# First two batches' queries and keys as six tokens to a partition on 96 partitions, second V ahead of the residual weights, third batch's key casts on ScalarE and its key transposes between the outputs

## Chip, cores, metric

One core of a Trainium2 chip. The metric is the device time of one execution in microseconds; a lower one is better. A kernel's time is the median of its runs; a profiled run adds its trace. In what follows faster or slower needs 2%.

## The reference

Attention in a window of 32 tokens to each side plus 8 global tokens, over 8 batches, 8 heads, 576 tokens of 64 columns; its output is the input of a gated feed-forward network with a residual:

```python
mask = (np.abs(pos[:, None] - pos[None, :]) <= 32) | is_global[:, None] | is_global[None, :]
x = softmax(where(mask, q @ k.T / 8, -1e9)) @ v           # 8 batches, 8 heads, 576 x 64
x = x.transpose(0, 2, 1, 3).reshape(4608, 512)
ffn = (gelu(x @ w_gate) * (x @ w_val)) @ w_out            # 512 -> 1536 -> 512
out = x + sigmoid(x @ w_res) * ffn
```

## The kernel before

It goes through the 4608 tokens in nine chunks of 512. Within a chunk TensorE makes the gate and value products (`g_ps`, `v_ps`), then the residual gate (`r_ps`, weights `wr_t`) and the output (`f_ps`, weights `wo_t`), and between these the scores and values of the next chunk. Global scores (`sg` from queries `qt`, `ss` from keys `kt`) of the next batch come at the end of a chunk's gate products. All weights are loaded in float32 and cast to bf16 in the first 75 us, mostly by GpSimd, in the same queue as the casts of Q, K and V. The first two batches are transposed by TensorE; from the third on, DMA transposes do it. An output product goes through two buffers: VectorE writes it to `prb`, GpSimd adds the residual into `ob`, and SyncE issues the store of `ob`; there are two of each. In the views PE is TensorE, POOL GpSimd, DVE VectorE, ACT ScalarE and SPq the queue of SyncE, which issues most transfers. The first two batches' Q and K were loaded per pair of heads, four tokens to each of 128 partitions, with a tail of 64 tokens (p < 0); the code is shortened:

```python
RPP = 4; SM = RPP * 128; ST = S - SM
def load_raw(b, what, p, eng):
    if p < 0:                                             # 64 tail tokens of all heads
        eng.dma_start(raw[b][what][:, MW:MW + RPP * D],
                      bass.AP(tensor=src.tensor, offset=..., ap=[[S * D, H], [RPP * D, ST // RPP], [1, RPP * D]]))
    else:                                                 # 512 tokens of two heads: 262 KB
        eng.dma_start(raw[b][what][:, PW * p:PW * p + PW].rearrange("c (h n) -> c h n", h=2),
                      src[b, 2 * p:2 * p + 2, 0:SM].rearrange("h (c r) d -> c h (r d)", r=RPP))
...
for p in (0, 1, 2, 3, -1):                                # second batch, after weight pieces 0 to 11
    for what in "kq": load_raw(1, what, p, nc.sync)
...                                                       # chunk 0, j == 5:
load_vraw(1); load_piece(14); load_piece(15)              # 12, 13 = wr_t were issued before
for n in (12, 13): cast_piece(n, POOL)
for c5 in range(5): cast_v(1, c5, POOL)
shift_v(1)
...                                                       # end of chunk 0, then chunk 1
for what in "kq": cast_second(what, POOL)                 # third batch: ten casts ahead of ...
    gpsimd.tensor_tensor(ob, prb, xtok, add)              # ... the four output adds, two prb buffers
    sync.dma_start(out, ob)
turn_qk(2); load_v(2); gather(...)                        # DMA transposes on SyncE, V on GpSimd
```

The softmax here doesn't subtract the row's maximum and nothing guards it: scores larger than these inputs give would overflow.

## Time and profile before

| | kernel before |
|---|---|
| median of the timed runs | 409.08 us (408.6 to 409.57) |
| the profiled run | 412.05 us, span 410.3 us, granted clock 0.996 |
| first gate product | 28.13 us |
| chunk 1 starts (gate product) | 75.75 us |
| chunk 2 starts | 123.04 us |
| chunk 2's start to the end | 287.3 us |

### The profile page before, as it was taken

The numbers are of one execution on the slowest core, as the hardware profiler recorded it, in microseconds if no ns is written. First come the engines' busy times: TensorE is split into PE (matmuls) and PEld (weight loads), VectorE is DVE, ScalarE is ACT, GpSimd is POOL, SyncE is SP. The second block draws the span as 40 slices with busy tenths as digits, with TensorE's granted clock in tenths as the row PEclk, the third lists the DMA queues.
The fourth block names the chain that finished last, engine by engine and source line by source line (L and its number), as shares of the span: only waits on it lengthen the run. The fifth ranks groups of instructions, "written<-read, shape, count | busy, mean of one in ns | idle before, by whom it ended". The sixth has DMA issues, their size and how long they took to land.

```text
span 410.3 us, 8005 instructions
## 1 busy us (share of the span) xinstructions
PE 389.0 (95%) x3136; PEld 204.7 (50%) x3136; DVE 201.2 (49%) x418; ACT 169.1 (41%) x278; POOL 170.8 (42%) x210
## 2 busy tenths in 40 slices
PE   2889999699999999999999999999999999999995
PEld 1554555244654465446544654456445644554442
DVE  6658537136544555345634563466336534463321
ACT  5674590023623363336333533353435343633320
POOL 6788685589326712562256215612600220021012
PEclk9999999989999999999999999999999999999999
DMA  7999999499939974999399938994692320031001
GB/s 228 219 386 355 220 289 240 114 154 170 140 89 113 196 64 88 125 155 115 92 115 168 111 91 108 161 125 81 104 133 54 76 67 0 2 91 54 1 26 77
DMA packets 151830, 53.28 MB, mean 130 GB/s; under 512 B 136368, under 2 KB 140976, under 8 KB 151792
## 3 DMA queue, kind: packets, MB, share of 16 engines
q1 hardware_dynamic: 75840, 42.41, 43.9%
q0 software_dynamic: 75392, 9.84, 37.5%
q8 instruction: 24, 0.39, 0.4%
q10 hardware_dynamic: 560, 0.52, 0.4%
q14 instruction: 14, 0.11, 0.1%
HBM read 39.19 MB, written 9.44 MB: 119 GB/s over the span
## 4 chain that ended last, share of the span: by engine, by line
PE 60%; issue 17%; DMA 12%; POOL 5%; SPq 5%; DVE 1%; POOLq 0%; ACTq 0%
PE v_ps L544 15%; PE g_ps L540 15%; PE f_ps L567 15%; PE r_ps L557 5%; SPq L177 3%; POOL ob L573 3%; PE nd L508 3%; DMA extra<-in_moe_w_val_dram 3%; DMA extra<-in_moe_w_out_dram 2%; DMA wo_t<-in_k_dram 2%; PE sc L464 2%; PE sn L441 2%; DMA ht<-in_q_dram 2%; PE nd L502 1%; PE sg L419 1%
## 5 line engine op out<-in xcount | busy, mean ns | idle before, releaser
L547 ACT ACTIVATE gsb<-g_ps 128x512 bf16<-128x512 f32 x108 | 64.5, 597 | 140.5 <-PE g_ps L540 135.7
L548 DVE SCALAR_TENSOR_TENSOR ht<-gsb,v_ps 128x512 bf16<-128x512 bf16 x108 | 74.0, 686 | 97.1 <-PE v_ps L544 94.2
L573 POOL TENSOR_TENSOR ob<-prb,xtok 128x512 f32<-128x512 f32 x36 | 41.5, 1153 | 187.2 <-DVE prb L571 186.1
L540 PE MATMUL g_ps<-xt,wg_t 128*128 128x512 bf16 x432 | 111.8, 381 | 4.2 <-DVE prb L571 3.5
L544 PE MATMUL v_ps<-xt,wv_t 128*128 128x512 bf16 x432 | 111.8, 381 | 0.1
L567 PE MATMUL f_ps<-wo_t,ht 128*128 128x512 bf16 x432 | 103.6, 379 | 1.0 <-POOL wo_t L137 1.0
L540 PEld LDWEIGHTS <-wg_t 128*128 128x128 bf16 x432 | 42.2, 98 | 54.5 <-issue 5.7
L544 PEld LDWEIGHTS <-wv_t 128*128 128x128 bf16 x432 | 42.5, 98 | 51.9 <-issue 1.6
L567 PEld LDWEIGHTS <-ht 128*128 128x128 bf16 x432 | 39.0, 98 | 40.1 <-issue 1.8
L560 ACT ACTIVATE rsb<-r_ps 128x512 bf16<-128x512 f32 x36 | 21.6, 604 | 74.1 <-PE r_ps L557 74.0
L571 DVE SCALAR_TENSOR_TENSOR prb<-rsb,f_ps 128x512 f32<-128x512 bf16 x36 | 24.7, 685 | 36.9 <-PE f_ps L567 28.7
L471 ACT ACTIVATE pt<-sc 128x512 bf16<-128x512 f32 x72 | 37.4, 610 | 4.0 <-PE sc L464 4.0
L557 PE MATMUL r_ps<-wr_t,xt 128*128 128x512 bf16 x144 | 36.8, 379 | 0.1
L486 DVE TENSOR_TENSOR pt<-pt,maskw 128x512 bf16<-128x512 bf16 x64 | 26.6, 428 | 9.0 <-ACT pt L471 6.9
L91 POOL DMA_DIRECT2D q_st<-in_q_dram x25 | 21.1, 862 | 21.8 <-DMA qt<-q_st 21.4
L99 POOL DMA_DIRECT2D ve<-in_v_dram x30 | 25.4, 862 | 0.0
L522 DVE TENSOR_TENSOR xtok<-nd,rden 128x512 bf16<-128x512 f32 x34 | 23.5, 691 | 1.3
L508 PEld LDWEIGHTS <-pt 128*128 128x128 bf16 x576 | 22.3, 97 | 1.0
L508 PE MATMUL nd<-ve,pt 128*128 128x65 bf16 x320 | 22.3, 193 | 0.0
L91 POOL DMA_DIRECT2D k_st<-in_k_dram x25 | 21.2, 875 | 2.7 <-DMA kt<-k_st 2.0
L521 DVE RECIPROCAL rden<-nd 128x8 f32<-128x8 f32 x34 | 7.0, 207 | 30.4 <-PE nd L508 30.2
L557 PEld LDWEIGHTS <-xt 128*128 128x128 bf16 x144 | 13.4, 97 | 15.1
(136 smaller groups left out, 306.1 us busy)
## 6 DMA issues: line engine op xcount, KB each, us to landing
out_dram<-ob SPq DMA_DIRECT2D x36, 256.0 KB, 2.1
vo<-ve SPq DMA_DIRECT2D x14, 260.0 KB, 5.6
q_st<-in_q_dram POOLq DMA_DIRECT2D x20, 128.0 KB, 5.2
k_st<-in_k_dram POOLq DMA_DIRECT2D x20, 128.0 KB, 6.4
ve<-in_v_dram POOLq DMA_DIRECT2D x18, 128.0 KB, 6.3
wo_t<-in_k_dram SPq DMA_DIRECT2D x8, 256.0 KB, 6.4
extra<-in_moe_w_gate_dram SPq DMA_DIRECT2D x4, 512.0 KB, 8.7
vraw<-in_q_dram SPq DMA_DIRECT2D x8, 256.0 KB, 6.4
```

What stands on the lines that cost most here:

```text
L91: nc.gpsimd.dma_start(dst[0:n, r, :].rearrange("p (h d) -> p h d", d=D), src[b].rearrange("h s d -> s h d")[128 * r:128 * r + n])
L99: nc.gpsimd.dma_start(t[p0:p1, c, :, 0:D], v[b].rearrange("h s d -> s h d")[s0 + p0:s0 + p1])
L471: nc.scalar.activation(mine, sc, ACTF.Exp, bias=0.0, scale=SCALE)
L486: nc.vector.tensor_tensor(m, m, view(maskw, 0, 128, 64 * i0, [[0, 2], [64, 4], [1, 64]]), ALU.mult)
L508: nc.tensor.matmul(nds[h // 4][:, VG * (h % 4):VG * (h % 4) + VG], view(pt, 0, 128, c0, [[1, 128]]), vw, start=False, stop=(h % 4 == 3 and ...
L540: nc.tensor.matmul(g_ps, wg_t[:, kk, 128 * j:128 * j + 128], x[:, kk, :], start=(kk == 0), stop=(kk == NKT - 1))
L544: nc.tensor.matmul(v_ps, wv_t[:, kk, 128 * j:128 * j + 128], x[:, kk, :], start=(kk == 0), stop=(kk == NKT - 1))
L547: nc.scalar.activation(gsb, g_ps, ACTF.Gelu, bias=0.0, scale=1.0)
L548: nc.vector.scalar_tensor_tensor(ht[:, j, :], gsb, 0.5, v_ps, ALU.mult, ALU.mult)
L557: nc.tensor.matmul(r_ps, xt[c % 2][:, kk, 128 * t:128 * t + 128], wr_t[:, kk, :], start=(kk == 0), stop=(kk == NKT - 1))
L567: nc.tensor.matmul(held["f"], ht[:, j, 128 * t:128 * t + 128], wo_t[:, j, :], start=(j == 0), stop=(j == NFF - 1))
L573: nc.gpsimd.tensor_tensor(ob, prb, xtok[c % 2][:, t, :], ALU.add)
```

## The change

Three parts. (1) Q and K of the first two batches are loaded as six tokens to each of 96 partitions, in eight loads of 295 KB, so the eight-head tail loads and their transposes and copies go. (2) The second batch's V is loaded and cast before the residual weights `wr_t`, so that `wo_t`, which waits behind the shift of V, comes earlier. (3) The third batch's keys are cast by ScalarE, so that only five query casts share GpSimd with the output adds, and the key transposes are issued on SyncE in the middle of the four outputs.

```diff
-    RPP = 4
-    SM = RPP * 128
+    RPP = 6
+    PC = S // RPP
...
-        if p < 0:
-            eng.dma_start(raw[b][what][:, MW:MW + RPP * D], ... 8 heads x 16 groups ...)
-        else:
-            eng.dma_start(raw[b][what][:, PW * p:PW * p + PW]..., src[b, 2 * p:2 * p + 2, 0:SM]...)
+        eng.dma_start(raw[b][what][0:PC, PW * p:PW * p + PW].rearrange("c (h n) -> c h n", h=2),
+                      src[b, 2 * p:2 * p + 2].rearrange("h (c r) d -> c h (r d)", r=RPP))
...
-    for n in (12, 13):
+    load_vraw(1)
+    for n in (12, 13, 14, 15):
         load_piece(n)
...
-                    load_vraw(1)
-                    for n in (14, 15):
-                        load_piece(n)
+                    for c5 in range(5):
+                        cast_v(1, c5, POOL)
+                        if c5 == 0:
+                            gather("k", 1)
+                    shift_v(1)
+                    gather("q", 1)
                     for n in (12, 13):
                         cast_piece(n, POOL)
-                    for c5 in range(5):
-                        cast_v(1, c5, POOL)
-                    shift_v(1)
+                    gather("v", 1)
...
-            for what in "kq":
-                cast_second(what, POOL)
+            cast_second("k", 0, NQT, ACT)
...
+            cast_second("q", 0, 1, POOL)
             work_f[3]()                      # output 1
+            turn_qk(2, "k")                  # five key transposes on SyncE
             values(1, 3)
+            cast_second("q", 1, 2, POOL)
             work_f[7]()                      # output 2
+            cast_second("q", 2, NQT, POOL)
...
-            turn_qk(b)
+            turn_qk(b, "q" if c == 1 else "qk")
```

More of the change, by code (lines that the diff above doesn't have):

```diff
@@ L64, in pair_of @@
         return [const.tile(shape, dt, name=f"{name}{i}", tag=f"{name}{i}") for i in range(2)]
-    q_st = const.tile([128, NQT, H * D], BF16, name="q_st", tag="q_st")
-    k_st = const.tile([128, NQT, H * D], BF16, name="k_st", tag="k_st")
+    q_st = const.tile([128, NQT + 1, H * D], BF16, name="q_st", tag="q_st")
+    k_st = const.tile([128, NQT + 1, H * D], BF16, name="k_st", tag="k_st")
     qt = pair_of([128, NP, S], "qt")
@@ L110, in flat32 @@
         return f.bitcast(F32)[:, o:o + 1024]
-    vraw = const.tile([128, 5, 512], F32, name="vraw", tag="vraw")
+    vraw = const.tile([128, 6, 512], F32, name="vraw", tag="vraw")
     extra = const.tile([128, 4, 1024], F32, name="extra", tag="extra")
@@ L137, in cast_piece @@
         copy(pieces[n][1], staged(n))
-    RPP = 4
-    SM = RPP * 128
-    ST = S - SM
+    RPP = 6
+    PC = S // RPP
     PW = 2 * RPP * D
-    MW = NP * PW
     ht32 = ht.rearrange("p a b -> p (a b)").bitcast(F32)
@@ L153, in load_raw @@
         src = {"q": q, "k": k}[what]
-        if p < 0:
-            eng.dma_start(raw[b][what][:, MW:MW + RPP * D],
-                          bass.AP(tensor=src.tensor, offset=src.offset + (b * H * S + SM) * D,
-                                  ap=[[S * D, H], [RPP * D, ST // RPP], [1, RPP * D]]))
-        else:
-            eng.dma_start(raw[b][what][:, PW * p:PW * p + PW].rearrange("c (h n) -> c h n", h=2),
-                          src[b, 2 * p:2 * p + 2, 0:SM].rearrange("h (c r) d -> c h (r d)", r=RPP))
-    for p in (0, 1, -1, 2, 3):
+        eng.dma_start(raw[b][what][0:PC, PW * p:PW * p + PW].rearrange("c (h n) -> c h n", h=2),
+                      src[b, 2 * p:2 * p + 2].rearrange("h (c r) d -> c h (r d)", r=RPP))
+    for p in range(NP):
         load_raw(0, "k", p, nc.sync)
@@ L185 @@
     place2 = {"q": [vraw[:, r, :] for r in range(NQT)],
-              "k": [extra[:, r // 2, 512 * (r % 2):512 * (r % 2) + 512] for r in range(NQT)]}
+              "k": [extra[:, r // 2, 512 * (r % 2):512 * (r % 2) + 512] for r in range(4)] + [vraw[:, 5, :]]}
     def load_second(what):
@@ L192, in load_second, with cast_second @@
                               {"q": q, "k": k}[what][2].rearrange("h s d -> s h d")[128 * r:128 * r + n])
-    def cast_second(what, copy):
-        for r in range(NQT):
+    def cast_second(what, r0, r1, copy):
+        for r in range(r0, r1):
             n = min(128, S - 128 * r)
@@ L260, in zero_globals, with staged_pair @@
         zero_wide(qgz[i], 0, 128, 0, [[1, NP * 16]])
+    def staged_pair(what, p):
+        return (q_st if what == "q" else k_st).rearrange("c a b -> c (a b)")[0:PC, PW * p:PW * p + PW]
     def cast_pair(b, p, what, copy):
-        big = (q_st if what == "q" else k_st)
-        if p < 0:
-            copy(big[:, RPP, :].rearrange("c (r t d) -> c r t d", t=2, d=D),
-                 view(raw[b][what], 0, 128, MW, [[D, RPP], [0, 2], [1, D]]))
-        else:
-            copy(big[:, p, :].rearrange("c (r u d) -> c r u d", r=RPP, u=2),
-                 raw[b][what][:, PW * p:PW * p + PW].rearrange("c (u r d) -> c r u d", u=2, r=RPP))
+        copy(staged_pair(what, p).rearrange("c (r u d) -> c r u d", r=RPP, u=2),
+             raw[b][what][0:PC, PW * p:PW * p + PW].rearrange("c (u r d) -> c r u d", u=2, r=RPP))
     hrow = const.tile([128, 1], I32, name="hrow", tag="hrow")
@@ L394, in turn_pair, with turn_qk @@
     def turn_pair(b, p, what):
-        src, dst, c0 = (q_st, qt[b], 0) if what == "q" else (k_st, kt[b], 32)
+        dst, c0 = (qt[b], 0) if what == "q" else (kt[b], 32)
         copy = nc.scalar.copy if what == "q" else nc.vector.tensor_copy
-        ps = pss.tile([128, RPP, 128], BF16, name=f"t{what}", tag="sc") if b else bank([128, RPP, 128], f"t{what}", BF16)
+        shape = [128, RPP, PC]
+        ps = pss.tile(shape, BF16, name=f"t{what}", tag="sc") if b else bank(shape, f"t{what}", BF16)
         for r in range(RPP):
-            nc.tensor.transpose(ps[:, r, :], src[:, p if p >= 0 else RPP, 128 * r:128 * r + 128], ident)
-        if p < 0:
-            CT = ST // RPP
-            for u in range(2):
-                got = view(ps, 64 * u, 64, CT * u, [[2 * CT, NP], [1, CT], [128, RPP]])
-                copy(dst[64 * u:64 * u + 64, :, c0 + SM:c0 + S].rearrange("c p (s r) -> c p s r", r=RPP), got)
-            return
-        copy(dst[:, p, c0:c0 + SM].rearrange("c (s r) -> c s r", r=RPP), ps.rearrange("c r s -> c s r"))
-    def turn_qk(b):
-        for src, dst, c0 in ((q_st, qt[b % 2], 0), (k_st, kt[b % 2], 32)):
+            nc.tensor.transpose(ps[:, r, :], staged_pair(what, p)[:, 128 * r:128 * r + 128], ident[0:PC, 0:PC])
+        copy(dst[:, p, c0:c0 + S].rearrange("c (s r) -> c s r", r=RPP), ps.rearrange("c r s -> c s r"))
+    def turn_qk(b, parts="qk"):
+        for what in parts:
+            src, dst, c0 = (q_st, qt[b % 2], 0) if what == "q" else (k_st, kt[b % 2], 32)
             for r in range(NQT):
@@ L592 @@
     cast_raw(1, "q", ACT)
-    for p in (-1, 2, 3):
+    for p in (2, 3):
         for what in "kq":
@@ L601 @@
     first_scores(0, 0)
-    for what in "kq":
-        turn_pair(0, -1, what)
     for what in "kq":
@@ L635 @@
             load_piece(10 + n)
-    for p in (0, 1, 2, 3, -1):
+    for p in range(NP):
         for what in "kq":
@@ L678 @@
                     hot_rows(1)
-                    for p in (0, 1, 2, 3, -1):
+                    for p in range(NP):
                         for what in "kq":
                             cast_pair(1, p, what, POOL)
-                    load_vraw(1)
-                    for n in (14, 15):
-                        load_piece(n)
+                    for c5 in range(5):
[4 more added lines that the diff above has]
+                    gather("q", 1)
                     for n in (12, 13):
                         cast_piece(n, POOL)
-                    for c5 in range(5):
-                        cast_v(1, c5, POOL)
-                    shift_v(1)
+                    gather("v", 1)
                     for n in range(16, 20):
                         load_piece(n)
-                    for what in "kqv":
-                        gather(what, 1)
                     for n in range(14, 20):
                         cast_piece(n, POOL)
-                if j > 6:
+                if 6 < j < 11:
                     for what in "kq":
-                        turn_pair(1, (0, 1, 2, 3, -1)[j - 7], what)
+                        turn_pair(1, j - 7, what)
             elif b < B:
@@ L729 @@
                 load_second(what)
-            for what in "kq":
-                cast_second(what, POOL)
+            cast_second("k", 0, NQT, ACT)
             work_f[1]()
```

## The prediction

> **What bounds the kernel now**
>
> I read the page first: busy tenths in 40 slices of 10.26 us.
>
> ```profile
> PE   2889999699999999999999999999999999999995
> POOL 6788685589326712562256215612600220021012
> PEclk9999999989999999999999999999999999999999
> DMA  7999999499939974999399938994692320031001
> ```
>
> TensorE (PE) is full from the fourth slice to the last but one, with one hole in slice 8 (72 to 82 us) and a low clock in slice 9, just after it. The DMA row dips in the same slice 8. Next, the table of stretches (length, then busy us of PE and the other engines; clock, DMA share and GB/s at the end):
>
> ```profile
> 28.00:82.00 54.00, 48.44 (x404) 25.93 (x404) 27.66 (x62) 22.93 (x40) 36.86 (x47) 1.00 0.91 251
> 86.50:406.00 319.50, 318.83 (x2478) 164.90 (x2475) 154.62 (x297) 126.74 (x207) 107.24 (x116) 1.00 0.81 98
> ```
>
> From 86.5 us on, PE idles 0.7 of 319.5 us. Nothing in the change removes matmuls there, so that part is a constant. What can be won lies before 86.5 us: the start (the first gate matmul is at 28.13 us) and the 5.6 us of idle in the first chunk. The list of PE's waits names these (us in total, times, longest); I show the three after 28.13 us that the change touches, the others there being 0.2 each:
>
> ```profile
> PE g_ps L540 <- DVE prb L571: 3.5, 1, 3.5
> PE f_ps L567 <- POOL wo_t L137: 1.0, 2, 0.8
> PE sg L419 <- ACT qt L404: 0.3, 1, 0.3
> ```
>
> The timeline of PE around the hole (start, duration, what, idle before):
>
> ```profile
> 75.75 1.03 PE L540 MATMUL g_ps<-xt,wg_t 128*128 128x512 bf16 x4
> 76.61 1.03 PE L544 MATMUL v_ps<-xt,wv_t 128*128 128x512 bf16 x4
> 81.18 1.02 PE L540 MATMUL g_ps<-xt,wg_t 128*128 128x512 bf16 x4 [3.54 <-DVE prb L571]
> 82.29 1.53 PE L544 MATMUL v_ps<-xt,wv_t 128*128 128x512 bf16 x4
> ...
> 86.56 1.03 PE L540 MATMUL g_ps<-xt,wg_t 128*128 128x512 bf16 x4
> ```
>
> Undisturbed groups of four start 0.863 us apart. The group at 81.18 was due at 77.47. The four groups from 81.18 to 86.56 took 5.38 us where 4 x 0.863 = 3.45 would do. So the hole costs 3.71 us and then 1.93 us at a low clock: 5.64 in all. The timelines of GpSimd (POOL) and VectorE (DVE) say why:
>
> ```profile
> 73.46 0.61 POOL L197 CAST k_st<-extra 64x512 bf16<-64x512 f32 x1 [1.35 <-DMA extra<-in_k_dram]
> ...
> 78.12 1.17 POOL L197 CAST q_st<-vraw 128x512 bf16<-128x512 f32 x2 [0.96 <-DMA vraw<-in_q_dram]
> 79.26 2.26 POOL L573 TENSOR_TENSOR ob<-prb,xtok 128x512 f32<-128x512 f32 x2
> ```
>
> ```profile
> 80.44 0.69 DVE L571 SCALAR_TENSOR_TENSOR prb<-rsb,f_ps 128x512 f32<-128x512 bf16 x1 [7.52 <-POOL ob L573]
> ```
>
> The two output products (prb) of 68.73 and 70.32 us sit in the only two prb buffers. GpSimd can add them to the residual only after ten casts of the third batch, each paced by its load, the last landing at 78.5. DVE then waits 7.5 us for a buffer and PE waits for the PSUM bank that DVE should have read. Hence the chain: third batch's loads, GpSimd casts, output add, PE.
>
> The loads are late because the DMA engines are the resource of the first 78 us. Two more stretches:
>
> ```profile
> 11.00:14.00 3.00, 3.00 (x37) 2.42 (x36) 1.53 (x4) 2.07 (x6) 1.79 (x4) 1.00 0.82 133
> 20.00:36.00 16.00, 13.66 (x145) 8.05 (x145) 9.75 (x30) 9.88 (x15) 13.57 (x16) 1.00 1.05 381
> ```
>
> Large weight rows move at 381 GB/s. At 11 to 14 us, behind the tail loads, it is 133, and the SyncE issue of one V load takes 3.52 us (9.60 to 13.12), one of the second V 5.02 us (from 42.36), where others take about 1.1.
>
> **What the Trainium skill says**
>
> "DMA: Bandwidth & Descriptors", section "Why a DMA increments its semaphore by 16 and not by 1": a transfer uses the largest number of engines up to 16 that divides the slowest dimension of both sides. The tail load's source starts with 8 heads, so 8 engines; 96 partitions give 16. The trace agrees: 9 completion marks for each tail, 16 for each other load of Q and K, and the weights behind the second tails land spread over 4.7 us (42.51 to 47.21) instead of 2.1.
>
> "SBUF — State Buffer", section "Door 1: The DMA port swizzle": 16 ports, eight of them for partitions 0 to 63. With 96 partitions these carry two thirds of the bytes. My estimate from its 27.2 GB/s a port: 295 KB x 2/3 / 8 / 27.2 = 0.90 us for a load, against 0.75 between landings for today's 262 KB. The trace of before has no such load.
>
> "TensorE: Matmul & The Clock Gate", Part 1: an idle window of about 3.4 us halves the clock. The trace agrees: after the 3.54 us gap the granted clock is one half for 3.41 us. The same page ("Architectural detail") calls GpSimd's queue a strict FIFO; the adds standing behind the casts agree.
>
> **The change part by part**
>
> 1. *Six tokens a partition, no tails.* Loads per batch: 8 of 256 KB plus 2 of 128 KB become 8 of 288 KB; the bytes are the same, but the eight loaded engines go from 10 to 9 units of 16 KB, and the other eight no longer idle. DMA per batch: 10 x 0.75 = 7.5 us on the slow engines becomes 8 x 0.79 to 0.90 = 6.3 to 7.2 (0.79 from 47 ns per 1024 B and 84 per 2048 B, hence 66 per 1536 B). The blocked V issues give more. I expect the DMA stream 2 to 5 us early by 50 us.
> PE, second batch: 40 transposes of 55 ns become 48 of 96 columns at about 42: 2.20 to 2.02, so -0.2. The wait on the tail copy (L404) goes, as the last turn now sits a step earlier: second half of sg at 52.07 instead of 51.57: -0.5.
> Start: the first casts grow from 512 to 768 columns (ACT 0.62 to 0.83, DVE 0.47 to about 0.65), and the first four loads carry an eighth more, so first scores come some 0.9 us later (10.24 to 11.1). Eight tail transposes, two copies of 0.43 and two of 0.37, and the wait for the last cast then go, which gives about 0.9 back by the global scores at 15.63. V no longer holds PE (the 0.94 us wait at 20.86), but ACT runs without a break from 17.29 to 23.87 and stays. Net at 28.13: -0.3 (+0.5 to -1).
>
> 2. *Second V ahead of the residual weights.* Order only. Its value is that wo_t's pieces, queued behind the shift of V, start earlier. In before PE waited for the wo_t casts: two pairs at 59.54 and 63.71 should have been 0.43 us and took 0.84 and 1.36: -1.3. Its price: wr_t is now cast after V and two gathers. PE needs it at 53.06 (51.8 after the gains so far). Estimate: weights done at 33 to 35.3, Q/K 40 to 42, V 5 x 1.15 more, wr_t 2 x 1.35: landed at 48.5 to 51, casts 2 x 1.04 done at 50 to 53. Between no wait and 1.3 us; I put +0.3.
>
> 3. *Third batch's keys on ScalarE.* Five casts of 0.61 leave GpSimd, and ACT, idle from 61.75 to 76.81, takes them at 0.62. The fifth key tile no longer waits for a slot of wo_t (SyncE stood 3.66 us). The adds now stand behind one, two and five query casts. Queries should land at 67 to 72, not 74 to 78.5, so the first add runs near 68 to 70 and no prb buffer is missed by 75: -3.7 of the hole, and with no hole no low clock: -1.9.
>
> Sum: -0.2 -0.5 -0.3 -1.3 +0.3 -5.6 = -7.6. 409.08 - 7.6 = 401.5 us, a ratio of 0.981.
>
> **Rivals**
>
> *wr_t becomes the wait.* For: it stands behind more work on GpSimd, and the 8-deep load queue was full. Against: DMA was held up by unbalanced engines. If so, +1 to +2.5: 402.5 to 404.
>
> *The hole only shrinks*, if 96 partitions run at the port limit and the queries land 3 us early at best: the first add is then at about 72, behind one cast, and PE loses 0 to 1 us but no clock: 402 to 402.5. Speaking against a full return of the hole: only one cast, not ten, stands ahead of the first add.
>
> *The start gains more*: V lands up to 3.5 us earlier, and if ACT's unbroken run begins sooner, the first gate matmul comes 1 to 1.7 us early: 400 to 400.8.
>
> *Nothing comes of it*, the loads being hidden: PE's 5.64 us speak against that.
>
> **Range and chances**
>
> Recovering the hole with its clock (5.6) is nearly safe, the 1.3 and 0.7 likely, the start and wr_t are worth about one us either way. Before's runs spread 1 us. Predicted 401.5, range 399.8 to 404.0. The 2% line is 400.9, 0.6 below: faster by over 2% 0.36, within 2% 0.63, slower 0.01.
>
> **What would show it**
>
> In the new profile: no PE wait on prb in the first chunk and no clock under 1 after it (step 3); no wait of f_ps on wo_t, and of r_ps on wr_t under 0.5 us (step 2); no V issue of several us on SyncE and landings of one load within about 2 us (step 1); first gate matmul at 27 to 28.5. Wrong would be: a new wait of more than 1.5 us on wr_t or on the second batch's casts, or a first gate matmul after 28.6, which would lose the gain; or one before 26.5, which would pass the line.

## More of the kernel before

All runs compared here are in the fast state, but for single looks, whose state isn't known and which are only read for their traces. One run of the kernel before (582 us, clock 0.66) was slow and is left out.

The chunk starts are read off the timeline of TensorE: the first `g_ps` after an `f_ps`. They cut the span into pieces that can be compared between kernels; the first chunk of the prediction and of the expectations is chunk 0, the second chunk 1.

## The result, and the profile after

| | before | after |
|---|---|---|
| median of the timed runs | 408.84 us (408.43 to 409.57, 4 runs) | 413.35 us (412.04 to 413.85, 4 runs) |
| ratio | | 1.0103, interval 1.0075 to 1.0131 |
| profiled run: time, span | 412.05, 410.3 us | 412.04, 410.3 us |
| first gate product | 28.13 | 28.48 |
| chunk 1 starts | 75.75 | 75.84 |
| chunk 2 starts | 123.04 | 122.80 |
| chunk 2's start to the end | 287.3 | 287.5 |

A ratio is the mean time of one kernel's fast runs over the mean of the other's fast runs of the same rounds, so it isn't quite the ratio of the medians. By the 2% rule the two are the same; the interval lies above 1, so the change made the kernel slower by about 1%, where I had predicted 1.9% less. The two profiled runs are equally long, because that of before is a long one of its kind and that of after the shortest of its four. They show what moved, not the size of it; a second profile of before, below, starts 1.8 us earlier.

The busy tenths of the page after (same rows as before):

```profile
PE   2989989996999999999999999999999999999994
POOL 7887854668626712562256215612600220021022
PEclk9999999999999999999999999999999999999999
DMA  8999999889939993999399938993991210031001
```

The hole of slice 8 is gone from the row of TensorE (PE), and so is the low clock in slice 9; but slice 10, 92 to 103 us, now has a 6. (A new stretch of low clock, below, lies across slices 10 and 11 and is too short in each to show in the row.) The list of PE's waits (total us, times, longest) says what took the hole's place:

```profile
PE sg L405 <- DMA qt<-q_st: 3.6, 2, 2.4
PE tq L390 <- ACT q_st L258: 3.3, 2, 2.2
PE r_ps L543 <- POOL wr_t L137: 1.5, 2, 1.1
...
PE g_ps L526 <- POOL wg_t L137: 0.7, 1, 0.7
```

There is no wait on prb and none of `f_ps` on `wo_t`: steps 3 and 2 took away what they should. There is a new wait on `wr_t`, and one that no line of the prediction has: on the DMA transposes of the third batch's queries, in chunk 1. The timeline of PE there, in which `v_ps` ends at 96.84:

```profile
95.81 1.03 PE L530 MATMUL v_ps<-xt,wv_t 128*128 128x512 bf16 x4
99.24 0.65 PE L405 MATMUL sg<-qt,kgz 128*128 128x288 bf16 x4 [2.40 <-DMA qt<-q_st]
101.08 1.12 PE L405 MATMUL sg<-qt,kgz 128*128 128x288 bf16 x4 [1.19 <-DMA qt<-q_st]
```

The table of stretches has a granted clock of one half (PEclk, third number from the end) for the 3.41 us that follow:

```profile
101.10:104.51 3.41, 3.19 (x33) 1.65 (x35) 0.45 (x1) 1.00 (x3) 3.41 (x6) 0.50 1.67 165
```

3.6 us of idle and, by my estimate, 1.7 us of half clock (half of 3.41): in this profile the old hole of 5.6 us has come back, 20 us later. SyncE's timeline tells where the queries' transposes were:

```profile
75.73 0.37 SPq L561 DMA_DIRECT2D out_dram<-ob  x1
76.65 6.56 SPq L399 DMA_TRANSPOSE kt<-k_st  x5
83.30 3.85 SPq L561 DMA_DIRECT2D out_dram<-ob  x3
87.20 6.95 SPq L399 DMA_TRANSPOSE qt<-q_st  x5
```

and GpSimd's (POOL) shows the same from its side:

```profile
74.55 1.15 POOL L559 TENSOR_TENSOR ob<-prb,xtok 128x512 f32<-128x512 f32 x1
...
79.09 1.15 POOL L559 TENSOR_TENSOR ob<-prb,xtok 128x512 f32<-128x512 f32 x1
85.64 1.15 POOL L559 TENSOR_TENSOR ob<-prb,xtok 128x512 f32<-128x512 f32 x1 [5.40 <-DMA out_dram<-ob]
86.73 4.32 POOL L99 DMA_DIRECT2D ve<-in_v_dram  x5
```

The first add runs at 74.55, behind one query cast, as intended. Then SyncE issues output 1, and after it five key transposes for 6.56 us. Outputs 2 to 4 stand behind them. There are two `ob` buffers, so the last add waits 5.40 us for one. Only then come V's loads on GpSimd and the query transposes on SyncE: at 87.20, where the kernel before, with its late adds, issued them at 85.38. PE arrives at `sg` at 96.84, 5.4 us earlier than before (102.21), and the last query tile lands at 101.04.

The other half of the plan, an earlier stream of loads, did not come about. Bytes moved per second, in 40 equal parts of 36 to 46 us, first before, then after:

```profile
GB/s 348 344 352 352 344 348 348 348 352 344 340 352 352 348 344 340 352 291 229 213 254 242 250 229 250 217 242 320 303 332 302 312 282 272 279 220 227 239 207 259
```

```profile
GB/s 270 258 264 295 276 264 252 295 289 252 252 295 283 264 252 277 301 270 264 252 289 295 276 207 263 264 249 219 218 214 194 174 180 70 62 197 194 260 254 157
```

Before, the second batch's loads run at some 350 GB/s until the tails come (from the 18th number, 40.3 us, on). After, they run at some 270 from the start. In the completion marks of the trace the first five of the eight new loads land 1.08 us apart (37.44, 38.52, 39.60, 40.68, 41.76) and the last at 44.77, 1.05 us apart in the mean, where I had put 0.79 to 0.90. What follows in the queue, V and `wr_t`, is all in at 53.66 us; in before it was 53.57. Of the 2 to 5 us to be gained, nothing.

### The profile page after: what moved, and what is told of

Its sections match the earlier page's. It is cut to its first block, busy times and chain, and to the rows that moved or that the text cites. A ratio compares the mean times of both kernels' runs of the same rounds, so it can differ in the third digit from the quotient of the medians.

```text
span 410.3 us, 7975 instructions
## 1 busy us (share of the span) xinstructions
PE 386.6 (94%) x3100; PEld 205.1 (50%) x3152; DVE 201.9 (49%) x414; ACT 171.9 (42%) x279; POOL 169.5 (41%) x201
## 3 DMA queue, kind: packets, MB, share of 16 engines
q1 hardware_dynamic: 74400, 42.35, 44.4%
## 4 chain that ended last, share of the span: by engine, by line
PE 78%; DMA 12%; issue 3%; SPq 2%; POOL 2%; DVE 2%; ACT 1%; POOLq 0%; ACTq 0%; DVEq 0%
PE f_ps L553 21%; PE v_ps L530 19%; PE g_ps L526 18%; PE r_ps L543 6%; PE nd L494 4%; DMA wo_t<-in_k_dram 3%; DMA vraw<-in_moe_w_out_dram 3%; PE sc L450 2%; DMA qt<-q_st 2%; PE nd L488 2%; PE sg L405 2%; DMA xt<-in_v_dram 2%; DMA ht<-in_q_dram 2%; PE sn L427 2%; SPq L399 1%
## 5 line engine op out<-in xcount | busy, mean ns | idle before, releaser
L526 PE MATMUL g_ps<-xt,wg_t 128*128 128x512 bf16 x416 | 108.9, 379 | 1.2 <-POOL wg_t L137 0.7
L553 PE MATMUL f_ps<-wo_t,ht 128*128 128x512 bf16 x407 | 100.6, 379 | 1.3
L472 DVE TENSOR_TENSOR pt<-pt,maskw 128x512 bf16<-128x512 bf16 x64 | 27.9, 453 | 10.8 <-ACT pt L457 8.9
L507 DVE RECIPROCAL rden<-nd 128x8 f32<-128x8 f32 x34 | 7.0, 207 | 28.7 <-PE nd L494 28.7
```

The costliest lines, as they stand in the source:

```text
L472: nc.vector.tensor_tensor(m, m, view(maskw, 0, 128, 64 * i0, [[0, 2], [64, 4], [1, 64]]), ALU.mult)
L526: nc.tensor.matmul(g_ps, wg_t[:, kk, 128 * j:128 * j + 128], x[:, kk, :], start=(kk == 0), stop=(kk == NKT - 1))
L553: nc.tensor.matmul(held["f"], ht[:, j, 128 * t:128 * t + 128], wo_t[:, j, :], start=(j == 0), stop=(j == NFF - 1))
```

## The experiments

Eighteen runs, all correct to the check against the reference. Two were wrong in the second batch, wide_six and ports_six: the reported result is not sharp enough to see it, so "correct" is not proof for those. Each is compared with runs of before on its own chip (medians 410.0 to 410.9 us).

| run | parts | key transposes | median us | ratio to before, interval |
|---|---|---|---|---|
| before_again | none | | 410.36 | 0.9996, 0.9963 to 1.0029 |
| after_again | 1 2 3 | amid the outputs | 412.59 | 1.0042, 0.9976 to 1.0108 |
| keys_late | 1 2 3 | behind the outputs | 409.35 | 0.9992, 0.9953 to 1.0032 |
| no_keys | 1 2 | | 412.65 | 1.0069, 1.0021 to 1.0117 |
| keys_only | 3 | amid | 406.76 | 0.9912, 0.9875 to 0.9949 |
| third_late | 3 | behind | 406.9 | 0.9913, 0.9857 to 0.9968 |
| order_late | 2 3 | behind | 406.16 | 0.9925, 0.9896 to 0.9955 |
| six_late | 1 3 | behind | 409.48 | 0.9983, 0.9959 to 1.0007 |
| six_only | 1 | | 416.14 | 1.0143, 1.0119 to 1.0167 |
| six_first | 1 (first batch) 3 | behind | 409.48 | 0.9951, 0.9897 to 1.0005 |
| six_second | 1 (second batch) 3 | behind | 409.7 | 0.9971, 0.9921 to 1.0021 |
| tails16_late | 3, tails on 16 engines | behind | 406.43 | 0.9903, 0.9847 to 0.9959 |
| best | the same, gathers moved | behind | 404.83 | 0.9882, 0.986 to 0.9904 |
| best_b | best again | behind | 405.32 | 0.9882, 0.985 to 0.9914 |
| best_order | best with 2 | behind | 409.71 | 0.9975, 0.9932 to 1.0017 |
| best_order_b | best with 2, again | behind | 406.4 | 0.9892, 0.9865 to 0.992 |

My theory after the result: the key transposes in the middle of the outputs give part 3's gain back, and part 1's loads are slow for their 96 partitions. The rival for the first: the gain was never there. For the second: the packets of 1536 B are slow, or the new order (part 2) makes the late `wr_t` alone.

### Is the difference real, and is part 3 worth anything: before_again, keys_late, no_keys, keys_only

before_again is the kernel before, unchanged.

> The kernel before, unchanged, as a control. Its profile had a 3.54 us hole on PE and then 3.41 us at half clock, yet its timed runs (408.4 to 409.6) lie some 3 us under the 412.05 of that profiled run. Clock theory: the low clock after the hole is a matter of luck[...], so typical runs have spans of 406.5 to 408 and a granted clock above 0.996, and the hole costs them 3.7 and not 5.6. If instead every run has the low clock, spans are 410 and clocks 0.996, and the 3 us are something else.

It measured 0.9996. Its profile has the same hole (wait on prb 3.6 us, half clock from 80.84 us), but its first gate product is at 26.34 us, not 28.13. In the trace that I predicted from, the second key load landed at 6.83 us; in other runs of that scheme at 4.8 to 5.4. So its start was 1.8 us later than here, by chance. The clock theory's first branch is missed: the four executions have a clock of 0.991 to 0.995, not above 0.996, and spans of 408.0 to 409.2 us. But the low clock is not in every run. One such stretch took the mean clock of the first profile to 0.996, and 8 of the 46 other fast runs of before that were taken beside the experiments have 0.997 or more.

keys_late takes the changed kernel and puts only the key transposes back:

```diff
-            turn_qk(2, "k")          # amid the outputs
...
-            turn_qk(b, "q" if c == 1 else "qk")
+            turn_qk(b)
```

> The changed kernel with one thing undone: the third batch's key transposes are no longer issued on SyncE between the first chunk's first and second output, but after all four, with the query transposes, as before. Order theory (the key transposes hold the outputs back by 6.6 us, so the last add, the third V and the query transposes start at 85.6 to 87.2 us, and PE, now 5.5 us ahead of where it was, waits 3.6 us at the global scores and then runs 3.4 us at half clock): the last add runs at about 81, transposes start at 82, queries are there by 94 and keys by 98, PE waits under 1.5 us, no low clock, 408 to 410 us timed. Stream theory (transposes, V and gathers share the DMA engines and need some 16 us from their start, whatever the order): keys land at 98 or later, PE waits 1 to 3 us for keys and the low clock may stay: 410 to 412. If the start of the kernel is the cause, nothing changes: 412 to 414.

SyncE's timeline of keys_late shows all outputs, then the queries, then the keys:

```profile
76.16 5.93 SPq L561 DMA_DIRECT2D out_dram<-ob  x4
82.19 6.66 SPq L399 DMA_TRANSPOSE qt<-q_st  x5
88.94 7.14 SPq L399 DMA_TRANSPOSE kt<-k_st  x5
```

The queries' transposes are issued 5.0 us earlier than in the changed kernel, PE's wait on `sg` is gone, and chunk 1 takes 42.2 us where it took 47.0 (44.4 in after_again). The chain read from the two timelines is confirmed. (In time it is less sure: 0.9992 and after_again's 1.0042 are from two chips, and their intervals overlap.) But chunk 0 takes 50.5 us here, for `wr_t` comes late. The waits and the stretch behind them:

```profile
PE r_ps L543 <- POOL wr_t L137: 3.7, 2, 2.6
```

```profile
55.45:58.86 3.41, 3.41 (x39) 1.47 (x38) 1.27 (x3) 2.57 (x5) 2.59 (x3) 0.50 1.03 273
```

no_keys undoes part 3 in the changed kernel (ten casts on GpSimd ahead of the adds); keys_only puts part 3 alone into before.

```diff
# no_keys, against after                          # keys_only, against before
-  cast_second("k", 0, NQT, ACT)                 -  for what in "kq": cast_second(what, POOL)
+  for what in "kq": cast_second(what, POOL)     +  cast_second("k", 0, NQT, ACT); casts of q between the outputs
-  turn_qk(2, "k") amid the outputs              +  turn_qk(2, "k") amid the outputs
```

> The changed kernel with its third part undone: keys cast by GpSimd ahead of the queries, all transposes after the outputs; six tokens a partition and the second V first stay. Order theory: the old hole at prb comes back nearly whole (its loads landed at 78.3 in the changed kernel against 78.5 before), and the wait at the global scores goes: about before's time plus the 1.5 us wait on the residual weights, less 1.8 us of gone waits: 408 to 410. If part 1 or 2 is what slows the kernel: 411 or more with no wait at the global scores.

> The kernel before with the third part alone: keys by ScalarE, early key transposes, queries cast between the adds. Order theory: the hole at prb goes and the wait on query transposes at the global scores comes, 3 us or more with the low clock after it: 410 to 413, slower than before. If part 1 or 2 is what slows the changed kernel: 404 to 406.

Parts 1 and 2 without 3 are slower than before by 0.7%, part 3 without 1 and 2 is faster by 0.9%, some 3.6 us. In keys_only the hole on prb is gone, no stretch of low clock is left, and chunk 1 takes 43.4 us. So part 3 is good and the loss sits in parts 1 and 2. The order theory is missed twice. It had 410 to 413 us for keys_only, which took 406.76. And it had the hole back nearly whole in no_keys, whose list of waits has no wait on prb above 0.2 us: `r_ps` waits 2.9 us for `wr_t` there, with a half-clock stretch from 57.15 us, so PE itself comes late (chunk 1 starts at 78.33). keys_only has its key transposes amid the outputs too; its wait on `sg` is 1.4 us in two pieces, without a low clock behind. Its queries landed 1.2 us earlier (77.06 against 78.27) and their transposes were issued 1.2 us earlier (85.98 against 87.20), but the second half of `sg` could start 3.5 us earlier (97.55 against 101.08). Why the transposes themselves took less time was not taken apart.

### Where do the transposes belong, and what do the tails cost: after_again, third_late, tails16_late, wide_six

after_again is the changed kernel, unchanged, on another chip. third_late is before with part 3 and the key transposes behind the outputs. tails16_late changes the order in which a tail load walks its source:

```diff
-  ap=[[S * D, H], [RPP * D, ST // RPP], [1, RPP * D]]      # 8 heads slowest
+  ap=[[RPP * D, ST // RPP], [S * D, H], [1, RPP * D]]      # 16 groups of 4 tokens slowest
...
-  got = view(ps, 64 * u, 64, CT * u, [[2 * CT, NP], [1, CT], [128, RPP]])
+  got = view(ps, 64 * u, 64, u, [[2, NP], [H, CT], [128, RPP]])
```

> The changed kernel, unchanged, beside the others and on their chip (before's runs of the two sessions so far differ by 2 us, 408.8 and 410.9). If the first session's ratio of 1.010 holds: 413 to 415. In the one profile seen the spans of both kernels were equal (410.3). Every run should have the low clock once or twice (granted clock 0.989 to 0.993), from the wait on the query transposes at 96.7 us and, in some runs, from the wait on the residual weights at 53 us.

> The kernel before with the third part (keys by ScalarE, queries cast between the adds), but with the key transposes left behind the outputs as before; no six tokens, no moved V. Order theory: first add near 73, no hole at prb; last add by 80, query transposes landed by 93, keys by 99; PE waits under 1 us at the global scores; second stage as in the run with late keys (42.2 us) instead of 43.4 with early ones and 47.3 before; 403 to 406 us, granted clock 0.997, faster than with early keys by about 1 us. Stream theory: the keys, now last, are the wait, and it equals early keys or is slower: 406.5 to 408.

> As the run before (third part with late key transposes), plus one edit in the tail loads of the first two batches: the source is walked token group first and head second, so that its slowest dimension is 16 and not 8; the tail then sits in other partitions and its copies pick them accordingly. If the tail loads cost because they use 8 of the 16 DMA engines: 16 completion marks for them, the spread of the weights' landings behind the second tails falls from 4.7 to about 2 us, no V issue of over 2 us on SyncE, the second V lands 1 to 2 us earlier, and the f_ps wait on wo_t shrinks: 0.5 to 1.5 us faster than without it. If the imbalance is harmless: the same time within 0.5 us.

after_again: 1.0042 here, 1.0103 on the first chip; slower in both, though the second interval holds 1. third_late equals keys_only (0.9913, 0.9912): that the late place is 1 us better, as I had expected, is missed. On this base the outputs come early enough for either; the place of the key transposes matters where the stream is late, which parts 1 and 2 make it. tails16_late: the tails now have 16 completion marks instead of 9, the weights behind them land spread over 2.2 us instead of 3.75, the last second V at 50.55 instead of 51.67, and the wait for `wo_t` is gone. Chunk 0 takes 46.4 us instead of 47.2; in time that is 0.1%, inside the interval. So the 8-engine tails, part 1's reason, cost some 0.8 us of this kernel's profile.

wide_six loads the second batch's rows of the changed kernel on 128 partitions, with the same packets of 1536 B. It reads the wrong tokens:

```diff
+  if b == 1:
+      eng.dma_start(raw[b][what][:, PW * p:PW * p + PW]..., ap=[[RPP * D, 128], [128 * RPP * D, 2], [1, RPP * D]])
```

> A measurement with a wrong result on purpose: the changed kernel, but the second batch's eight loads of Q and K go to 128 partitions, two rows of 1536 bytes to each (393 KB a load, some rows read twice), instead of 96 (295 KB). In the changed kernel such a load took 1.08 us (273 GB/s) and one packet of 1536 bytes 96 ns, more than one of 2048 bytes of the weights (87 ns). Port theory (96 partitions put two thirds of the bytes on half of the SBUF ports): with 128 partitions the packet falls to about 66 to 70 ns and the load to 1.05 to 1.1 us for a third more bytes, 360 GB/s or more. Packet theory (1536 bytes are slow in themselves): 96 ns stay, 1.5 us a load, 273 GB/s.

In the completion marks its loads of 393 KB land 1.05 us apart, as long as 295 KB took on 96 partitions. The rate over 36 to 44 us:

```profile
GB/s 361 384 384 384 353 384 369 376 369 369 369 392 369 361 376 369 369 376 376 376 353 392 384 361 384 353 376 376 376 371 334 304 285 270 173 149 154 147 224 175
```

Packets of 1536 B run at some 370 GB/s here. They are not the cause. A third more bytes on a third more partitions cost no time; so the missing 32 partitions save none.

### Which part costs: six_late, order_late, six_only

Against third_late: six_late has part 1 as well, order_late has part 2 as well. six_only is before with part 1 alone. Their edits are the blocks of the change's diff.

> The changed kernel with part 2 undone and the key transposes behind the four outputs: parts 1 and 3. Theory (the order of part 2 makes the wait on the residual weights): no wait of r_ps on wr_t above 0.3 us (3.7 with part 2), no low clock behind it, first chunk 47.0 to 47.8 us (50.5 with part 2), second chunk 42.2 to 44.3, time 0.990 to 0.993 of before, as the same without part 1. Rival (the 96-partition loads make that wait, because they are slower each): r_ps waits over 1 us for wr_t here too and the time is 0.997 or more of before.

> Before with parts 2 and 3, key transposes behind the outputs, loads of Q and K as in before (128 partitions and tails). Theory (order alone makes the wait): r_ps waits 1.5 to 3.7 us for wr_t, with a half-clock stretch of 3.41 us behind it in some runs, first chunk 49 to 50.5 us, no wait of f_ps on wo_t, second chunk 42 to 44.3, time 0.996 to 1.001 of before. Rival (six tokens a partition are part of the cause): no wait on wr_t above 0.5 us, first chunk about 46.5, time at most 0.991.

> Before with part 1 alone. My theory now (a load of 96 partitions takes 1.08 us and the stream gains nothing): the last query of the third batch lands within 1 us of 78.5 minus 1.5, VectorE's wait for a prb buffer and with it the hole of PE of 2.5 to 4 us stay, first chunk 47.2 to 48.8, time 0.998 to 1.004 of before. The predicted theory (the stream is 2 to 5 us early): queries land by 75, hole under 1 us, no low clock, time 0.990 or less.

My theory had blamed the order, and it falls. order_late waits 0.9 us for `wr_t` in two pieces with no low clock, and runs at 0.9925, by its interval no different from third_late's 0.9913. six_late has no wait on `wr_t`, as I had said, but its time is 0.9983 and not 0.990 to 0.993: 0.7% is lost with part 1 in whichever order (0.9983 against 0.9913, 0.9992 against 0.9925). Each of these pairs is from two chips and their intervals overlap slightly; those of six_late and order_late, on one chip, lie just apart. The third_late waits, then those of six_late:

```profile
PE ss L425 <- DMA kt<-k_st: 1.3, 1, 1.3
PE tq L399 <- ACT q_st L268: 1.1, 2, 0.8
...
PE f_ps L568 <- POOL wo_t L137: 0.8, 2, 0.6
```

```profile
PE tq L390 <- ACT q_st L258: 3.5, 2, 1.9
PE f_ps L553 <- POOL wo_t L137: 2.9, 3, 2.0
PE ss L410 <- DMA kt<-k_st: 1.6, 2, 0.9
```

With part 1 the wait moves to whatever stands last in the stream: `wo_t` with the old order (the second V landed at 55.99 us, in third_late at 51.67), `wr_t` with the new one (landed at 54.18 in keys_late, 51.45 in order_late). And part 1 alone is the slowest kernel of all, 1.0143: its third batch comes later still, behind ten casts, and PE waits in chunk 1:

```profile
103.82 0.26 PE L410 MATMUL ss<-qgz,kt 128*128 128x16 bf16 x4 [2.82 <-DMA kt<-k_st]
105.28 0.28 PE L410 MATMUL ss<-qgz,kt 128*128 128x16 bf16 x4 [1.21 <-DMA kt<-k_st]
```

The clock is at one half from 104.14 for 6.83 us. The hole on prb shrank to 0.9 us, only because PE itself was late: the predicted theory for six_only, 0.990 or less, is refuted. My own 0.998 to 1.004 is missed too, on the slow side. (Why 1.0143 is more than no_keys' 1.0069 was not taken apart; they ran on two chips.)

### Why 96 partitions are slow, and which batch pays: ports_six, six_first, six_second

ports_six takes six_late and loads 64 of the 96 groups of the second batch: the keys to partitions 0 to 63, the queries, the same 196 KB, as two transfers to 0 to 31 and to 64 to 95.

```diff
+  for p0, n in ((0, 64),) if what == "k" else ((0, 32), (64, 32)):
+      eng.dma_start(raw[b][what][p0:p0 + n, ...], src[b, 2 * p:2 * p + 2, RPP * p0:RPP * (p0 + n)]...)
```

> A measurement of the loads, wrong on purpose for the second batch: parts 1 and 3, where the second batch's keys load 64 of the 96 chunks as one transfer to partitions 0 to 63 and its queries the same bytes (196 KB) as two transfers to partitions 0 to 31 and 64 to 95; all keys first, then all queries. Theory (the eight ports of partitions 0 to 63 set the time; 96 partitions in a row put on each of these as much as 128 would): a key load takes 0.95 to 1.25 us between landings, as 96 and 128 partitions of the same row length did, and a query load of two halves 0.50 to 0.65. Rival (packets of 1536 B are slow, wherever they go): both take 0.72 to 0.83, two thirds of the 1.08 to 1.25 of 96 partitions.

The rate over 35 to 43 us (from about 38.4 us on many records of packets are missing from this trace, so only the first 17 numbers, all of them the keys', are to be read):

```profile
GB/s 205 189 205 210 190 205 189 207 207 200 192 200 218 207 215 192 161 277 138 31 85 215 215 62 38 15 215 238 54 31 61 200 230 108 38 77 184 292 110 154
```

By the completion marks, which are complete, the keys land at 38.22, 39.25, 40.23 and 41.17 (0.98 us each, 200 GB/s), and the pairs of query halves are in at 41.79, 42.34, 42.90, 43.44 (0.55 us each, 357 GB/s). The same bytes and the same packets: partitions 0 to 63 take 1.8 times as long as 32 from each half. The rival (0.72 to 0.83 for both) falls. What sets the time of a load here is how much the partitions below 64 get: 64 rows of 3072 B took 0.98, 96 rows 1.05 to 1.25 in the mean of a run's eight loads, 128 rows 1.05. (The query loads were also cut into two transfers; that this alone makes them faster was not tested.)

six_first and six_second give part 1 to one batch only, on third_late.

> Before with part 3 (key transposes behind the outputs) and six tokens a partition for the first batch only; the second batch loads as in before. Part 1 for both batches cost 0.7% on top of part 3 (0.9983 against 0.9913). Theory (both batches pay, because a load of 96 partitions is slow: 1.24 us each at the start): first gate matmul at 28.3 to 28.6 us (26.1 without part 1), second V landed about 1.4 us later than the 51.7 of before with part 3, first chunk 47.0 to 47.9, time 0.994 to 0.997. Rival (only the start pays): the whole 0.7% is here, time 0.998. Second rival (only the stream of the second batch pays): first gate matmul at 26 to 27, time 0.991.

> Before with part 3 (key transposes behind the outputs) and six tokens a partition for the second batch only. Theory (both batches pay): first gate matmul at 25.9 to 26.3 us, the eight loads land 1.1 to 1.25 us apart, second V landed at 53.2 to 54.6 (51.7 without part 1), f_ps waits 1.5 to 3 us for wo_t, time 0.993 to 0.996. Rival (only the start pays): no more wait for wo_t than 0.8, time 0.991. Second rival (only this stream pays): 0.998.

Both lie between third_late and six_late, 0.9951 and 0.9971, with intervals too wide to rank them; that each pays some 0.4% fits, that one pays all is not excluded by time. Nor is the chip: third_late was not run on this one, and best_order, which has no part 1 at all, came out 0.8% slower on it than on another (see below). So the times of these two runs show little. The traces show the stream's share: in six_second the eight loads land 1.2 us apart and the second V at 55.11 us (I had said 53.2 to 54.6; 52.70 in six_first, 51.67 in third_late), and PE waits 1.9 us for `wo_t`, with a half-clock stretch of 3.41 us behind it. Its start was late without part 1 in the first batch (28.31 us): a miss for my expectation. PE has a gap of 1.5 us there for which the profile shows no releaser, of the kind that best_order shows below; so this start says nothing on part 1.

### A version that beats both: best, best_order, best_b, best_order_b

best is tails16_late with the six gathers for the later batches, which are not needed before chunk 2, taken away from the moment at which the third batch's transposes are on their way:

```diff
             load_v(b)
-            if c == 1:
-                for n in range(2, B // 2):
-                    for what in "kqv": gather(what, n)
...
                         load_qk(b + 1)                  # chunk 1, j == 8
+                    if c == 1: (the same six gathers)
```

best_order adds part 2 to it. Both were run twice, the second time on one chip.

> Before with part 3, key transposes behind the outputs, the tail loads with the token groups as the slowest dimension (16 engines), and the six gathers of the later global rows moved in the second chunk from its start to behind the loads of the fourth batch. Theory (the transposes of the third batch land late because the gathers and V loads share the DMA engines with them): the wait of ss on kt of 1.2 us goes to 0.4 or less, second chunk 42.3 to 43 (43.5 before this edit), time 0.984 to 0.990 of before. Rival (the transposes are paced by their own issue on SyncE, 1.3 to 1.4 us each): the wait stays at 1 us or more, second chunk 43.5, time 0.990; or the loads of the fourth batch now take the place of the gathers and nothing changes.

> The best so far (part 3 with late key transposes, tails with the token groups slowest, gathers moved; 0.988 of before) with part 2 as well: second V ahead of the residual weights. Theory (part 2 by itself costs a short wait for wr_t and saves the wait for wo_t and so about nothing): r_ps waits 0.3 to 1.5 us for wr_t, no wait of f_ps on wo_t above 0.2 (0.8 in the best), first chunk 46.5 to 47.8, time 0.985 to 0.989. Rival: wr_t comes in time now that the tails use 16 engines, and the time is 0.984 or less.

> The best version again (part 3 with late key transposes, tails with the token groups slowest, gathers moved), on one chip with its twin that has part 2 as well: 0.986 to 0.991 of before if the first measurement (0.9882) was no accident of its chip; above 0.994 if it was.

> The best version with part 2, again: its first run (0.9975) had two gaps of 1.17 us in TensorE's stream with no releaser in the profile, in a stretch that part 2 does not touch, and no run on the other chips had such a gap. Theory (those gaps are the chip's, part 2 is worth about nothing): 0.985 to 0.992, within 0.4% of its twin, r_ps waiting 0.5 to 1.5 us for wr_t. Rival (part 2 costs in this kernel): 0.5% or more above the twin here too.

In its first run best did as the theory says: the wait of `ss` on the key transposes went from 1.2 to 0.4 us, chunk 1 from 43.5 to 42.25. In the profile of best_b that wait is 1.4 us and chunk 1 takes 43.5, so the edit's mechanism isn't settled; the time is 0.9882 both times, 1.2% below before. That the tails and the gathers add anything to part 3 is not shown: third_late's 0.9913 lies within 0.4%, and the intervals overlap.

best_order's first run, 0.9975, looked as though part 2 cost 0.9%. Its PE timeline has gaps that no wait explains, in a stretch that the edit doesn't touch:

```profile
105.74 0.25 PE L465 MATMUL sc<-qt,kt 64*128 64x64 bf16 x4 [1.17 <-issue]
107.17 0.39 PE L465 MATMUL sc<-qt,kt 64*128 64x64 bf16 x14 [1.17 <-issue]
```

("issue": PE waited for nothing that the profile shows.) Gaps of this kind above 0.3 us were found in all four kernels of that call, on that one chip, and in none of the other profiles. On another chip, best_order_b ran at 0.9892 beside its twin's 0.9882: part 2 is worth nothing either way, within about 0.4%. That the gaps belong to the chip is not shown beyond this.

## Why the prediction was wrong, by its own steps

**Part 1, the loads: the step that failed.** "8 x 0.79 to 0.90", and from it "the DMA stream 2 to 5 us early by 50 us". Measured: 1.05 to 1.08 us in the changed kernel, 1.22 to 1.25 in the mean in six_late, six_only and six_second. With equal order, the second V lands 3.4 to 4.3 us later than without part 1 (55.11 to 55.99 against 51.67), not earlier. I had the right mechanism (two thirds of the bytes go to the half of the ports that serves partitions 0 to 63) and a wrong rate for it: I took the skill's 27.2 GB/s a port, though the trace of before had the number. Its loads spread evenly over 16 ports, 262 KB in 0.75 us, which is 16.4 KB a port, 21.8 KB per us. The new load puts 295 x 2/3 / 8 = 24.6 KB on each loaded port, and 24.6 / 21.8 is 1.13 us. Eight of these are 9.0 us against 7.5 for the ten old loads, so 1.5 us *later* per batch, before any run. This is the same bytes a port as for 128 partitions, which is just what wide_six showed. It is an estimate all the same: in ports_six the eight ports under the keys gave 25.1 KB per us each (196.6 KB / 8 in 0.98 us), so a port has no single rate, and the measured 1.05 to 1.25 lie on both sides of 1.13. The prediction's own figures made the loads only 0.3 to 1.2 us shorter per batch; most of its 2 to 5 us rested on the other half of the step, that V's issues on SyncE would no longer stall. That fell too: 3.73 and 4.30 us in the changed kernel, 3.86 and 5.36 in six_only, where third_late has 3.00 and 4.57. They were mostly not the tails' doing: with tails on 16 engines (tails16_late) they are still 2.53 and 3.83.

**The start, "-0.3".** Against the profile that I had, it came out at +0.35 (28.48). Against before in general it is worse: the first gate product is at 28.3 to 28.7 us in seven of nine profiles with part 1 in the first batch (26.86 and 29.99 the others), and in eleven without it the median is 26.15, with two above 27.2. The catch-up I counted on did not come. ScalarE's two query casts, before_again and then six_only:

```profile
5.62 0.62 ACT L268 CAST q_st<-ht 128x512 bf16<-128x512 f32 x1
...
7.42 0.62 ACT L268 CAST q_st<-ht 128x512 bf16<-128x512 f32 x1
```

```profile
6.51 0.83 ACT L258 CAST q_st<-ht 96x768 bf16<-96x768 f32 x1 [1.01 <-DMA ht<-in_q_dram]
...
9.71 0.83 ACT L258 CAST q_st<-ht 96x768 bf16<-96x768 f32 x1 [0.98 <-DMA ht<-in_q_dram]
```

The second is 2.3 us later, waiting for its load. The clock is granted in full from 18.5 to 19.9 us in seven of these nine, against 11.7 to 14.5 in ten of the eleven others, which is the other part of the loss. The profile of keys_late separates the two by chance: its second query cast is as late (9.50 us), yet the clock is full from 14.48, and the first gate product comes at 26.86. So of the two us and more the late clock takes some 1.6 (26.86 against 28.48 in the changed kernel) and the late cast some 0.7 (against the median of 26.15). That the late cast makes a late clock more likely is my reading, and not shown.

**Part 2.** The wait on the tail copy (-0.5) went, and "no wait of f_ps on wo_t" (-1.3) came true: neither wait is in the list after. "+0.3" for `wr_t` was too small: 1.5 and 2.5 us in the two profiles of the changed kernel, 3.7 in keys_late, in two of these with a half-clock stretch behind, which costs 1.7 more by the same estimate. The rival "wr_t becomes the wait" named it with 1 to 2.5 us. But the order alone was not its cause: in order_late, the same order without part 1, it is 0.9. The late stream made the rest.

**Part 3.** The hole went, with its low clock, and for the reason given: one cast ahead of the first add instead of ten. Not by the loads: the queries landed at 73.85 to 78.27 us, not at 67 to 72. Alone it was worth 0.9%, 3.6 us, of the predicted 5.6.

**"That part is a constant."** This is the second step that failed. From 86.5 us on I had found 0.7 us of idle and taken it for safe. From chunk 2's start it was: 287.3 to 287.7 us in every kernel. Chunk 1 was not. It was quiet in before because PE, held up in the hole, came late enough for transposes that ended just in time. I read the diff's key transposes as "moved" and did not ask what stands behind them on SyncE: three outputs, through their buffers GpSimd's last add, V's loads, and the queries' transposes. Of the predicted 7.6 us the changed kernel's profile lost again 3.6 + 1.7 here, 1.5 on `wr_t`, and the earlier loads altogether.

## What to carry to other kernels

Size a load by what its busiest port gets, at the rate that your own trace shows for an even load; 96 partitions in a row took at least as long as 128 (1.05 to 1.25 us against 1.05). When a wait is taken away, follow every in-order queue for the next chunk and ask whether what the engine needs there comes earlier too; a stretch without idle time may only be quiet because the engine came late. And compare the profiled run's time with the timed ones before using its first microseconds as a base: the start of this kernel scattered by 2 to 3 us between runs.

## What the Trainium skill lacked or had wrong

- "SBUF — State Buffer", section "Door 1: The DMA port swizzle": its ports explain the loads here, but its table has no row for 96 partitions (1.05 to 1.25 us for 295 KB here). Its 27.2 GB/s a port is an asymptote, as the page itself says (its 1 MiB reading for all 16 ports is 328 GB/s), and should not have been used for loads of this size: here a port got 21.8 with all ports even (262 KB in 0.75 us), 23.4 in wide_six (393 KB in 1.05 us) and 25.1 with half of them in use (196.6 KB in 0.98 us).
- The same page, section "Can I just issue two DMAs to hit both halves?", answers no, with 6% gained. Here two queued transfers to partitions 0 to 31 and 64 to 95 moved 196 KB in 0.55 us, against 0.98 us for one transfer to 0 to 63.
- "TensorE: Matmul & The Clock Gate", Part 1, speaks of an idle window of about 3.4 us; for shorter gaps it says only that frequent small ones can make the clock swing, without a length. Here the clock was halved after two gaps with work between them: 2.40 and 1.19 us (the changed kernel), 2.58 and 1.10 (keys_late), 0.83 and 1.68 (after_again), 1.55 and 0.39 (six_second). After 2.05, 0.39 and 0.46 us (six_late), spread over some 7 us, it was not.
- On no page: gaps of TensorE without a releaser, twice 1.17 us in one run and once 1.5 in another, on one chip of several.
